# Attention phases of eight scores, with scores and products sharing seven PSUM banks

## The chip, the core and the metric

The kernel runs on one core of one Trainium2 chip. The metric is device time in microseconds (us) of that core; the time before is 1309.45 us, the median of three runs (1308.44 to 1309.51). Five engines run their own instruction streams and meet at semaphores: TensorE (PE in the profile; PEld is its loading of weights), ScalarE (ACT), VectorE (DVE), GpSimd (POOL) and SyncE (SP), which issues the DMAs. Matmul results land in PSUM, which has eight banks of 128 x 512 float32.

## What is computed

One input x (2048 tokens x 512 channels) goes through attention and through a token-mixing MLP, and a gate mixes the two:

```python
qkv = (x @ wqkv)            # 32 heads of 16 channels
p = softmax(q k^T / 4)      # per head, 2048 x 2048
a = (p v) @ wo
h = layernorm(x)
b = (W2 gelu(W1 h^T + b1) + b2)^T     # over the tokens, 1792 hidden
out = g * a + (1 - g) * b   # g = sigmoid(sum(x * gate_w))
```

## The kernel before

The first 300 us project v, q and k, and run the first layer of the MLP. From there to the end of the attention (line 783 to 867) one loop does three things side by side on TensorE: the scores, the products with v, and "dense" matmuls, which are the second MLP layer and later the output projection with wo.

**Groups.** The attention is cut into 32 groups: two halves of the queries (1024 each) times 16 pairs of heads. A group has 64 scores. One score (`score`, the matmul of line 804) is a 128-key by 512-query tile of one head. It uses 64 rows of the array, so a score of head i=0 and one of head i=1 run at the same time on the two halves of the rows; a dense matmul is cut into two halves of 64 rows, which run beside a score in the same way. Two such matmuls that run beside each other are called a slot below.

**From score to product.** Two scores go into one PSUM tile `s` of two banks (three such tiles, line 529). ScalarE takes both in one exponential of 128 x 1024 (line 813) into an SBUF tile `pt`, of which there are six (line 527). Then `apply_v` multiplies by v (line 768): each score gives two matmuls of 17 columns (16 channels and a column of ones for the softmax's sum), 256 wide, on one of four blocks of 32 columns of the array. They add up in one PSUM bank `av` over the whole group (line 531). One more bank, `dn`, holds the dense result.

**Phases.** A group runs in ten phases of six scores and one of four. In a phase TensorE first issues the scores with the dense halves beside them, then all products with v of the *previous* phase's scores. A "two" is a pair of phases; its dense matmuls do one half of their rows in the first phase and the other half in the second. The function `put` deals out how many dense matmuls a two has: 80 of the 160 twos have six (a phase then has six slots), 79 have four (five slots, since two of the six scores then run beside each other) and one has eight. Between the last dense matmul of a phase and the first of the next stands a one-element memset on GpSimd (`token`, line 848).

**Around it.** At the end of a group VectorE copies `av` to the SBUF (`evacuate`, line 731) and later, from a list `slow` that gives out one piece of work per two, takes the reciprocal of the sums (line 742). Both go to DRAM. `fetch_o` (line 596) brings four pairs of heads back, and VectorE multiplies values by reciprocals (line 608) and splits the product in a high and a low part for the output projection. VectorE also evacuates `dn` (lines 513 and 628) and rounds the MLP's weights (line 65), and GpSimd subtracts (line 66). All of these queues are in the order in which the program issues them.

Of the kernel before, what the change touches and what calls it, by code (L numbers as in the profile page):

```python
# [9 lines left out]
F32 = mybir.dt.float32  # L10
# [3 lines left out]
AF = mybir.ActivationFunctionType  # L14
# [7 lines left out]
P = 128  # L22
# [36 lines left out]
def gated_mix(ctx: ExitStack, tc: tile.TileContext, a_x, a_wqkv, a_wo, b_w1, b_b1, b_w2, b_b2, gate_w, out):  # L59
# [3 lines left out]
    def split(hi, lo, src, copy, sub):  # L63

        copy(hi, src)  # L65
        return sub(lo, src, hi.bitcast(F32), ALU.subtract)  # L66
# [456 lines left out]

    o_d = [[dram.tile([P, QW], F32, name=f"o{h}{k}") for k in range(ND)] for h in range(2)]
# [71 lines left out]
    def fetch_o(half, k, pairs=4):  # L596

        n = pairs * 2
        pool, name, bufs = (end, str(k), 1) if half and k > 1 else (o_pool, "", 2)
        rb = pool.tile([P, QW], F32, name=f"o_sum{name}", bufs=1)[: n * DH]  # L600
# [4 lines left out]
        nc.sync.dma_start(rb, r_d[half][k][:n, None, :].broadcast_to([n, DH, QW]))  # L605

        def divide():
            nc.vector.tensor_mul(rb, raw, rb)
            split(hi, lo, rb, nc.vector.tensor_copy, nc.vector.tensor_tensor)

        slow.append((two + 1, divide))
        o_parts[half, k] = hi, lo
# [46 lines left out]
    TWOS = 5  # L659
# [9 lines left out]
    def call(at, *what):  # L669
        calls.setdefault(at, []).append(what)  # L670

    def put_outputs(tiles, n, m, at, sizes=None):
        for t in tiles:
            steps, load = project(t, n, m)
            call(at - 1, load)
            at = put(steps, at, sizes or [m - n])
        return at

    def sizes_of(at, n, fours):

        sizes = [6] * n
        for i in [i for i in reversed(range(n)) if (at + i) % TWOS][:fours]:
            sizes[i] = 4
        return sizes
# [7 lines left out]
    for t in range(NS):  # L692
        if t:
            at = put(second_layer(t), at, sizes_of(at, 9, 6) if t > 9 else sizes_of(at, 8, 3))
# [4 lines left out]
        if t == 10:  # L699
            call(at - 8, fetch_o, 0, 2)  # L700
            call(at - 5, fetch_o, 0, 3)
            at = put_outputs(range(NH), 6, 12, at)
    call(at - 8, fetch_o, 1, 0)
    call(at - 5, fetch_o, 1, 1)
    assert at - 5 > (NP + 8) * TWOS + 4
    call(at, open_end)
    at = put_outputs(range(NS - 3, NS), 0, 4, at)
    assert at == (NP + 12) * TWOS + 7
    call(at - 3, fetch_o, 1, 2)
    at = put_outputs(range(NH, NS - 3), 0, EARLY, at, [4, 4])  # L710
    at = put_outputs(range(NS - 3, NS), 4, EARLY, at)
# [4 lines left out]
    av = ps_av.tile([P, NB], F32, name="av")  # L716
    nc.vector.memset(av, 0.0)
# [7 lines left out]
    def evacuate(g):  # L725
        ot = out_pool.tile([P, NB], F32, name="ot")
        if g == NG - 1:
            for x, y in zip(column_halves(ot), column_halves(av)):
                nc.vector.tensor_scalar_max(x, y, least[0])
            return ot  # L730
        nc.vector.tensor_copy(ot, av)  # L731
# [7 lines left out]
        def invert():  # L739
            rt = out_pool.tile([P, NB], F32, name="rt", bufs=1)  # L740
            nc.vector.tensor_scalar_max(rt, ot, LEAST_SUM)
            nc.vector.reciprocal(rt, rt)  # L742

            def store():
                for rows, cols in blocks:
                    dst = r_d[half][k][None, 2 * p : 2 * (p + 1), cols]
                    nc.sync.dma_start(dst, rt[rows][DH:].rearrange("r (i n) -> r i n", i=2))

            stores.append(store)

        slow.insert(0, (two, invert))

    added = [0, 0]

    def pairs_of(g, units, last):

        pairs = list(zip(*([u for u in units if u[2] == qb] for qb in range(2))))
        return [(g, pair, last and n == len(pairs) - 1) for n, pair in enumerate(pairs)]

    def apply_v(pairs):  # L760
        ot = None
        for g, pair, last in pairs:
            for i, c, qb, pt in pair:

                added[qb] += 1
                for h in range(2):
                    j = 2 * qb + h
                    nc.tensor.matmul(  # L768
                        av[32 * j : 32 * j + VC, i * QC : (i + 1) * QC],
                        v[:, c, g % NP * 2 + i, :],  # L770
                        pt[:, h * QC : (h + 1) * QC],
                        start=added[qb] == 1,
                        stop=added[qb] == 2 * NS,
                    )
            if last:
                added[:] = 0, 0
                ot = evacuate(g)
        return ot

    engines = {getattr(mybir.EngineType, name) for name in ("PE", "Activation", "DVE", "Pool", "SP")}  # L780
    with tc.manual_schedule(engines=engines):
        kt, qt = {0: load_k(0)}, {0: load_q(0)}
        late, open_s, fence = [], None, None
# [9 lines left out]
        def score(grp, i, n, done):  # L793

            nonlocal open_s
            c, qb = n // 2, (n + i) % 2
            if open_s is None:
                open_s = ps_s.tile([P, 2, NB], F32, name="s"), ptp.tile([P, 2, NB], F32, name="pt")
                m = 0
            else:  # L800
                m = 1
            s, pt = open_s
            rows = slice(i * HALF, i * HALF + ROWS)
            nc.tensor.matmul(  # L804
                s[:, m, :],
                kt[grp][rows, c * P : (c + 1) * P],
                qt[grp][rows, qb * NB : (qb + 1) * NB],
                start=True,
                stop=True,
            )  # L810
            done.append((i, c, qb, pt[:, m, :]))
            if m:
                nc.scalar.activation(pt, s, AF.Exp, scale=SCALE)  # L813
                open_s = None

        for grp in range(NG):
            at = [0, 0]
            for ph in range(2 * TWOS + 1):
# [6 lines left out]
                if ph == 2 * TWOS:  # L825
                    n_s, beside = 4, []
                elif second:
                    n_s = 6
                else:
                    for what, *args in calls.get(two, ()):  # L830
                        what(*args)
                    n_s, beside = 6, [step(*args) for step, *args in dense.get(two, ())]
                units = []
                for n in range(n_s - len(beside)):
                    i = (n + second + 1) % 2
                    score(grp, i, at[i], units)
                    at[i] += 1
                half = slice(0, HALF) if second else slice(HALF, P)
                for m, (ps, a, b, first, last, done) in enumerate(beside):

                    if not 4 <= m < len(beside) - 2 or len(beside) <= n_s:
                        score(grp, second, at[second], units)
                        at[second] += 1
# [6 lines left out]
                    if done and second:  # L850
                        done()
                if grp == ph == 0:
                    shift_rows(nc.vector, k_bufs[1])
                if second:
                    while stores:
                        stores.pop()()
                    if len(ready) < 2:
                        split_weight(nc.vector.tensor_copy)
                    for n, (ready_at, step) in enumerate(slow):
                        if ready_at <= two:  # L860
                            slow.pop(n)[1]()
                            break
# [10 lines left out]
    with (  # L873
# [3 lines left out]
        pa = [ps_end.tile([P, D], F32, name=f"pa{t}") for t in range(8)]  # L877
# [153 lines left out]
```

## Time and profile before

| What | Value |
|---|---|
| Median of three runs | 1309.45 us |
| The profiled execution's own time | 1307.55 us |
| Its span, first to last instruction | 1305.8 us |
| Before the attention loop's first score | 303.1 us |
| Attention loop, to the end of the last exponential | 984.2 us |
| After it | 18.4 us |

The profiled execution is 1.9 us under the median and inside 0.15% of it. The profile's page gives busy time of each engine, the chain of work that ended last, and the costliest groups of instructions. In a group's row stand the line, the engine, the operation, output and inputs with their shapes and how often it ran; then the busy time in us and the mean duration in ns, and then the idle time of the engine ahead of it with what ended that. In a timeline each row has the start in us, the time to the end of the last instruction that the row merges, and in brackets the idle time ahead of it. Matmuls overlap in the records, so that TensorE reads as busy nearly all the time; how fast it goes is read from the distance between starts.

### The profile page before, as it was taken

To read this page: it belongs to the slowest core of one execution; us is meant where nothing else is said; L and a number is where in the kernel's file an instruction comes from. 1 tells how busy PE (TensorE), PEld (TensorE's weight loads), DVE (VectorE), ACT (ScalarE), POOL (GpSimd) and SP (SyncE) were. 2 spreads that over 40 slices of the span, in tenths; PEclk is the share of its full clock that TensorE was granted. 3 is DMA by queue.
4 is the path that set the end of the run, shared out by engine and by line. 5 is a ranking of instruction groups with operands and counts; after the bars stand their busy time and mean duration, and the time that the engine had idled before them with its cause. 6 is when DMAs were issued, how large, how long until landed. Compare 5 with 4: busy or idle time off the path is not lost.

```text
span 1305.8 us, 32289 instructions
## 1 busy us (share of the span) xinstructions
PE 1299.0 (99%) x13282; PEld 764.3 (59%) x13282; DVE 403.9 (31%) x538; ACT 1090.6 (84%) x1248; POOL 200.0 (15%) x467
## 2 busy tenths in 40 slices
PE   9999999999999999999999999999999999999998
PEld 7888888886555555555555555555555555454444
DVE  5775361445121111122322111232111111233324
ACT  3443343448999999999999999999999999999994
POOL 0210244453101011011000111100010101100000
PEclk9999999999999999999999999999999999999999
DMA  4497643337443333334655443545433333365522
GB/s 129 144 308 275 229 117 97 97 88 148 75 86 66 62 75 84 69 75 90 126 113 121 82 76 72 120 115 118 79 67 63 74 62 77 75 123 115 112 64 74
DMA packets 93384, 138.41 MB, mean 106 GB/s; under 512 B 14293, under 2 KB 53355, under 8 KB 90156
## 3 DMA queue, kind: packets, MB, share of 16 engines
q1 hardware_dynamic: 92652, 135.20, 44.3%
q8 instruction: 107, 1.75, 0.6%
q10 hardware_dynamic: 576, 1.05, 0.2%
q14 instruction: 49, 0.40, 0.1%
HBM read 99.63 MB, written 36.56 MB: 104 GB/s over the span
## 4 chain that ended last, share of the span: by engine, by line
PE 99%; DVE 0%; issue 0%
PE av L768 37%; PE s L804 29%; PE acc L412 12%; PE acc L73 10%; PE dn L844 10%; PE pa L887 1%; PE acc L184 1%; PE dn L789 0%; PE acc L251 0%; PE acc L228 0%; PE pa L917 0%; DVE base L930 0%; PE pa L895 0%; PE pa L894 0%; DVE idle L223 0%; PE acc L210 0%
## 5 line engine op out<-in xcount | busy, mean ns | idle before, releaser
L813 ACT ACTIVATE pt<-s 128x1024 f32<-128x1024 f32 x1024 | 962.5, 1025 | 20.9 <-PE s L804 14.9
L804 PE MATMUL s<-qs,ks 64*128 64x512 f32 x2048 | 521.3, 420 | 0.0
L768 PE MATMUL av<-pt,v 128*17 128x256 f32 x8192 | 510.6, 381 | 0.0
L804 PEld LDWEIGHTS s<-qs,ks 64*128 64x128 f32 x2048 | 297.6, 184 | 207.6 <-ACT pt L813 182.8
L768 PEld LDWEIGHTS av<-pt,v 128*17 128x17 f32 x8192 | 205.3, 97 | 259.5 <-issue 119.2
L844 PE MATMUL dn<-u_hi,w_hi 64*128 64x512 f32 x428 | 179.6, 420 | 0.0
L844 PE MATMUL dn<-u_hi,w_lo 64*128 64x512 f32 x430 | 170.2, 396 | 0.0
L844 PE MATMUL dn<-u_lo,w_hi 64*128 64x512 f32 x430 | 170.1, 396 | 0.0
L66 POOL TENSOR_TENSOR w_lo<-w_raw,w_hi 128x512 fp32r<-128x512 f32 (+1 forms) x126 | 151.7, 1205 | 115.1 <-ACT w_hi L65 108.5
L848 POOL MEMSET token<- 1x1 f32 x320 | 29.9, 93 | 873.3 <-PE dn L844 704.1
L731 DVE COPY ot<-av 128x512 f32<-128x512 f32 x31 | 21.5, 692 | 344.9 <-PE av L768 344.9
L65 ACT CAST w_hi<-w_raw 128x512 fp32r<-128x512 f32 (+1 forms) x67 | 38.1, 569 | 79.6 <-PE acc L412 58.8
L742 DVE RECIPROCAL rt<-rt 128x512 f32<-128x512 f32 x31 | 104.0, 3353 | 1.1
L412 PE MATMUL acc<-h_hi,w_hi 128*128 128x512 f32 x224 | 87.1, 389 | 0.0
L412 PE MATMUL acc<-h_lo,w_hi 128*128 128x512 f32 x224 | 87.1, 389 | 0.0
L412 PE MATMUL acc<-h_hi,w_lo 128*128 128x512 f32 x224 | 87.1, 389 | 0.0
L65 DVE CAST w_hi<-w_raw 128x512 fp32r<-128x512 f32 (+1 forms) x61 | 23.5, 387 | 190.2 <-PE s L804 82.0
L844 PEld LDWEIGHTS dn<-u_lo,w_hi 64*128 64x128 f32 x430 | 79.5, 185 | 2.5 <-POOL token L848 0.2
L844 PEld LDWEIGHTS dn<-u_hi,w_lo 64*128 64x128 f32 x430 | 79.4, 185 | 2.6
L844 PEld LDWEIGHTS dn<-u_hi,w_hi 64*128 64x128 f32 x428 | 78.8, 184 | 2.2
L73 PE MATMUL acc<-xt_hi,wc_hi 128*128 128x512 f32 x128 | 49.8, 389 | 0.0
L73 PE MATMUL acc<-xt_lo,wc_hi 128*128 128x512 f32 x128 | 49.8, 389 | 0.0
(142 smaller groups left out, 1001.5 us busy)
## 6 DMA issues: line engine op xcount, KB each, us to landing
w_raw<-in_B_w_dram SPq DMA_DIRECT2D x96, 256.0 KB
ks<-kp SPq DMA_DIRECT2D x192, 128.0 KB
qs<-qp SPq DMA_DIRECT2D x256, 64.0 KB
qp<-pc SPq DMA_DIRECT2D x16, 768.0 KB
x<-in_A_x_dram SPq DMA_DIRECT2D x32, 256.0 KB
kp<-pc SPq DMA_DIRECT2D x16, 512.0 KB
w_raw<-in_B_w_dram SPq DMA_DIRECT2D x32, 128.0 KB
bp<-row SPq DMA_DIRECT2D x16, 256.0 KB
```

What stands on the lines that cost most here:

```text
L65: copy(hi, src)
L66: return sub(lo, src, hi.bitcast(F32), ALU.subtract)
L73: nc.tensor.matmul(ps, a, b, start=start and n == 0, stop=stop and n == last)
L184: nc.tensor.transpose(turns[t][:, k, :], xs[t][:, k * P : (k + 1) * P], ident)
L412: nc.tensor.matmul(p, a, b, start=first and k == 0, stop=last and k == 2)
L731: nc.vector.tensor_copy(ot, av)
L742: nc.vector.reciprocal(rt, rt)
L768: nc.tensor.matmul(av[32 * j : 32 * j + VC, i * QC : (i + 1) * QC], v[:, c, g % NP * 2 + i, :], pt[:, h * QC : (h + 1) * QC], start=added[ ...
L804: nc.tensor.matmul(s[:, m, :], kt[grp][rows, c * P : (c + 1) * P], qt[grp][rows, qb * NB : (qb + 1) * NB], start=True, stop=True,)
L813: nc.scalar.activation(pt, s, AF.Exp, scale=SCALE)
L844: mm = nc.tensor.matmul(ps, a[half], b[half], start=first and not second, stop=last and bool(second))
L848: fence = nc.gpsimd.memset(token, 0.0)
```

## The change

Phases have eight scores, and a group has eight of them (`TWOS = 4`, `N_S = 8`). A two has six or eight dense matmuls and none has four. There are 128 twos; 18 of them have eight dense matmuls and 110 have six, so 36 phases have eight dense halves (eight slots) and 220 have six (seven slots, the first with two scores beside each other).

The three two-bank tiles and the bank `av` become one tile of seven banks. A table `TURN` says for each of eight phases, which repeat, into which banks its eight scores go and into which bank the products of that phase go. Two scores in neighbouring banks are taken by one exponential of 128 x 1024. In every fourth phase the last two scores are not neighbours and are taken by two exponentials of 128 x 512. The products of one phase are added up in their bank, and VectorE then adds that bank to an SBUF tile `ot` (`sums`), which GpSimd has set to zero at the start of the group. Only the parts of the bank that the phase has written are added: in a phase with six dense halves two instructions (128 x 256 and 64 x 256), with eight one (128 x 256). The copy at the group's end goes. `reads` and `writes` set the waits by bank: a matmul waits for what last read its bank, a reader waits for the matmuls that wrote it.

The reciprocals are cut in two halves, and the division of `fetch_o` in two pieces; `slow` is now looked at once per phase, and not in phases that round weights or end a dense tile. The output projection is dealt out in 24 runs instead of 27. The pool of `pt` tiles keeps its six tiles.

```diff
+    RING = 7
+    TURN = [
+        ((3, 4, 5, 6, 0, 1, 2, 3), 4),
+        ((5, 6, 0, 1, 2, 3, 4, 5), 6),
+        ((0, 1, 2, 3, 4, 5, 6, 0), 1),
+        ((4, 5, 2, 3, 0, 6, 1, 5), 4),
+    ]
+    TURN += [(tuple(RING - 1 - s for s in scores), RING - 1 - b) for scores, b in TURN]
...
     ptp = ptp_ctx.enter_context(tc.tile_pool(name="pt", bufs=6, reuse_waits="tile"))
-    ps_s = psum_ctx.enter_context(tc.tile_pool(name="ps_s", bufs=3, space=PSUM, reuse_waits="tile"))
+    ps_s = psum_ctx.enter_context(tc.tile_pool(name="ps_s", bufs=1, space=PSUM, reuse_waits="tile"))
-    ps_av = psum_ctx.enter_context(tc.tile_pool(name="ps_av", bufs=1, space=PSUM, reuse_waits="tile"))
...
-        slow.append((two + 1, divide))
+        slow.append((two + 1, lambda: nc.vector.tensor_mul(rb, raw, rb)))
+        slow.append((two + 1, lambda: split(hi, lo, rb, nc.vector.tensor_copy, nc.vector.tensor_tensor)))
...
-    TWOS = 5
+    TWOS = 4
+    N_S = 8
...
+    banks = ps_s.tile([P, RING, NB], F32, name="s")
...
+    def reads(ins, *at):
...
+        for bank in at:
+            readers[bank].append(ins)
+            for mm in writers[bank].values():
+                tc.add_manual_dep(ins.ins, mm.ins.name, SYNC, reason="the bank is written")
+
+    def writes(mm, bank, block=0, source=None):
...
+        for ins in readers[bank]:
+            tc.add_manual_dep(mm.ins, ins.ins.name, SYNC, reason="the bank is read")
+        readers[bank].clear()
...
+    def apply_v(late, bank, end=False):
...
+        pairs = [sorted(units[n : n + 2], key=lambda u: u[2]) for n in range(0, N_S, 2)]
+        av = banks[:, bank, :]
...
+        for x, y in parts:
+            reads(nc.vector.tensor_tensor(x, y, x, ALU.add), bank)
...
+            beside = [m for m, unit in enumerate(units) if unit[3] is None and abs(turn[m] - bank) == 1]
+            if beside:
+                exponentials(turn, units, [sorted((beside[0], len(units) - 1), key=lambda m: turn[m])])
+            elif len(units) == N_S:
+                exponentials(turn, units, [[m] for m, unit in enumerate(units) if unit[3] is None])
+
+        def exponentials(turn, units, runs):
+            pt = ptp.tile([P, 2, NB], F32, name="pt")
...
+                act = nc.scalar.activation(dst, banks[:, at[0] : at[-1] + 1, :], AF.Exp, scale=SCALE)
+                reads(act, *at)
...
-            for ph in range(2 * TWOS + 1):
+            for ph in range(2 * TWOS):
+                if ph == 0:
+                    sums[grp] = out_pool.tile([P, NB], F32, name="ot")
+                    nc.gpsimd.memset(sums[grp], 0.0)
...
+                turn, av_bank = TURN[(2 * two + second) % len(TURN)]
...
-                n = 2 if ph == 2 * TWOS and grp < NG - 1 else len(late)
-                apply_v(late[:n])
-                late = late[n:] + pairs_of(grp, units, ph == 2 * TWOS)
-        last_ot = apply_v(late)
+                apply_v(late, av_bank)
+                if grp and not ph:
+                    store_sums(grp - 1)
+                late = grp, units
```

More of the change, by code (lines that the diff above doesn't have):

```diff
@@ L1 @@
+from collections import deque
 from contextlib import ExitStack
@@ L598, in fetch_o @@
         n = pairs * 2
-        pool, name, bufs = (end, str(k), 1) if half and k > 1 else (o_pool, "", 2)
-        rb = pool.tile([P, QW], F32, name=f"o_sum{name}", bufs=1)[: n * DH]
+        assert stored.issuperset(half * NP + 4 * k + p for p in range(pairs))
+        pool, name, bufs = (end, str(k), 1) if half else (o_pool, "", 2)
+        rb = pool.tile([P, QW], F32, name="o_sum", bufs=1)[: n * DH]
         hi = pool.tile([P, QW], F32R, name=f"o_hi{name}", bufs=bufs)[: n * DH]
@@ L723, in column_halves, with store_sums @@
         return x[:, 0], x[:, 1]
[L725 to L731, printed above, removed]
+    def store_sums(g):
+        ot = sums.pop(g)
         half, p = divmod(g, NP)
@@ L737, in evacuate, with invert, store @@
             nc.sync.dma_start(dst, ot[rows][:DH].rearrange("r (i n) -> r i n", i=2))
[L739 to L765, printed above, removed]
+        rt = []
+        def invert(i):
+            if not rt:
+                rt.append(out_pool.tile([P, NB], F32, name="rt", bufs=1))
+            cols = slice(i * QC, (i + 1) * QC)
+            nc.vector.tensor_scalar_max(rt[0][:, cols], ot[:, cols], LEAST_SUM)
+            nc.vector.reciprocal(rt[0][:, cols], rt[0][:, cols])
+        def store():
+            stored.add(g)
+            for rows, cols in blocks:
+                dst = r_d[half][k][None, 2 * p : 2 * (p + 1), cols]
+                nc.sync.dma_start(dst, rt[0][rows][DH:].rearrange("r (i n) -> r i n", i=2))
+        slow[:0] = (two, lambda: invert(0)), (two, lambda: (invert(1), stores.append(store)))
+    def apply_v(late, bank, end=False):
+        if not late:
+            return
+        g, units = late
+        pairs = [sorted(units[n : n + 2], key=lambda u: u[2]) for n in range(0, N_S, 2)]
+        av = banks[:, bank, :]
+        taken = [0, 0]
+        for pair in pairs:
+            for i, c, qb, pt, act in pair:
+                taken[qb] += 1
                 for h in range(2):
                     j = 2 * qb + h
-                    nc.tensor.matmul(
+                    mm = nc.tensor.matmul(
                         av[32 * j : 32 * j + VC, i * QC : (i + 1) * QC],
@@ L851, in gated_mix @@
                         done()
+                if splits:
+                    split_weight(nc.vector.tensor_copy)
                 if grp == ph == 0:
                     shift_rows(nc.vector, k_bufs[1])
[L854 to L862, printed above, removed]
-                n = 2 if ph == 2 * TWOS and grp < NG - 1 else len(late)
-                apply_v(late[:n])
-                late = late[n:] + pairs_of(grp, units, ph == 2 * TWOS)
-        last_ot = apply_v(late)
+                apply_v(late, av_bank)
+                if grp and not ph:
+                    store_sums(grp - 1)
+                late = grp, units
+        assert not slow and not stores
+        last_ot = sums[NG - 1]
+        apply_v(late, TURN[0][1], end=True)
     psum_ctx.close()
@@ L876, in gated_mix @@
     ):
-        pa = [ps_end.tile([P, D], F32, name=f"pa{t}") for t in range(8)]
+        pa = {t: ps_end.tile([P, D], F32, name=f"pa{t}") for t in (7, 2, 4, 6, 1, 3, 5, 0)}
         LATE = 3, 5, 7
```

129 lines of the change are left out of this document (70 added, 59 removed).

## The prediction

> **What bounds the kernel now.** I read the page first (sections 1, 2, 4 and 5), then busy time by stage, then the waits of ScalarE and of the weight loads, then the timeline of three neighbouring phases on TensorE and ScalarE.
>
> ```profile
> span 1305.8 us, 32289 instructions
> PE 1299.0 (99%) x13282; PEld 764.3 (59%) x13282; DVE 403.9 (31%) x538; ACT 1090.6 (84%) x1248; POOL 200.0 (15%) x467
> PEclk9999999999999999999999999999999999999999
> PE 99%; DVE 0%; issue 0%
> L813 ACT ACTIVATE pt<-s 128x1024 f32<-128x1024 f32 x1024 | 962.5, 1025 | 20.9 <-PE s L804 14.9
> ```
> ```profile
> 303.20:1287.40 984.20, 984.20 (x11840) 508.11 (x11840) 229.34 (x241) 963.06 (x1025) 100.89 (x381) 1.00 0.43 88
> 1287.40:1305.80 18.40, 12.77 (x95) 8.72 (x92) 11.03 (x16) 1.09 (x2) 1.29 (x1) 0.92 0.34 120
> ```
>
> The chain is TensorE throughout, at full granted clock. The stage row is the attention loop: 984.2 us, columns PE, PEld, DVE, ACT, POOL. ScalarE is busy 963 us of it, so two engines are close to full, and a change in how they wait for each other decides. VectorE has 755 us free.
>
> The timeline of TensorE from 856.20 holds a phase with five slots, the group's four-score phase and one with six slots; below it is ScalarE.
>
> ```profile
> 856.20 0.50 PE L804 MATMUL s<-qs,ks 64*128 64x512 f32 x2
> 856.54 0.63 PE L804 MATMUL s<-qs,ks 64*128 64x512 f32 x2
> 857.01 0.40 PE L804 MATMUL s<-qs,ks 64*128 64x512 f32 x1
> 857.24 0.39 PE L804 MATMUL s<-qs,ks 64*128 64x512 f32 x1
> 857.57 1.49 PE L768 MATMUL av<-pt,v 128*17 128x256 f32 x24
> 858.99 0.73 PE L804 MATMUL s<-qs,ks 64*128 64x512 f32 x4
> 859.66 1.06 PE L768 MATMUL av<-pt,v 128*17 128x256 f32 x16
> 860.64 0.50 PE L804 MATMUL s<-qs,ks 64*128 64x512 f32 x1
> 862.25 1.49 PE L768 MATMUL av<-pt,v 128*17 128x256 f32 x24
> 863.67 0.49 PE L804 MATMUL s<-qs,ks 64*128 64x512 f32 x1
> ```
> ```profile
> 856.80 1.03 ACT L813 ACTIVATE pt<-s 128x1024 f32<-128x1024 f32 x1
> 861.47 2.86 ACT L813 ACTIVATE pt<-s 128x1024 f32<-128x1024 f32 x3
> 864.49 1.02 ACT L813 ACTIVATE pt<-s 128x1024 f32<-128x1024 f32 x1 [0.17 <-PE s L804]
> ```
>
> From these starts: five slots take 858.99 - 856.20 = 2.79 us, six take 863.67 - 860.64 = 3.03, the four-score phase 1.65. With 160, 159 and 31 of them that is 485 + 444 + 51 = 980 us, the stage within half a per cent: TensorE sets the pace of every phase. ScalarE does three exponentials in 2.86 us, an interval of (2.86 - 1.03) / 2 = 0.915, or 2.75 per phase, and then waits for the next phase's first scores (0.17 idle at 864.49). Its queue never runs dry for longer, and TensorE waits for no bank for long, since a score's bank was read by the exponential three before.
>
> **The change, part by part.** *TensorE's own work.* Slots start 0.23 apart after a first one of 0.34 (856.20, 856.54; 857.01, 857.24), and the products follow the last slot's start by 0.33 (857.24 to 857.57). The products of six scores take 1.42 (857.57 to 858.99), of four 0.98, so eight take 1.42 + 0.43 = 1.85. A phase of seven slots is then 1.37 (five slots) + 2 x 0.23 + 1.85 = 3.68, one of eight 3.91. With 220 and 36 phases: 810 + 141 = 951 us, 33 less than now; this is what going from 352 phases to 256 takes off the switches between scores and products. Matmul counts stay.
>
> *ScalarE's own work.* 256 phases of four intervals are 937 us. The 64 phases with two exponentials of 512 columns have no row. From the rows below, 512 columns take 0.59 to 0.69 us where 1024 take 1.03; bounds for the interval are 0.46 (half of 0.915) and 0.69 (no overlap). I take 0.50, as the shorter row saves 0.44 of 1.03 and 0.915 - 0.44 = 0.48. A pair then costs 0.085 more than one of 1024 (bounds 0 and 0.47): 5 us, so 942.
>
> ```profile
> L65 ACT CAST pc<-acc 128x512 fp32r<-128x512 f32 x32 | 18.7, 585 | 23.8 <-PE acc L73 19.3 <-DMA qp<-pc 4.6
> L351 ACT ACTIVATE pc<-acc,kmax 128x512 fp32r<-128x512 f32 x16 | 11.0, 689 | 14.2 <-DVE pc L66 14.2
> ```
>
> Either engine alone would be faster than 984. But the table adds two waits between them, and both lie on a loop that closes once per phase.
>
> *The eighth score's bank.* In every row of `TURN` the eighth score goes into a bank of the first pair (3 in 3,4; 5 in 5,6; 0 in 0,1; 5 in 4,5). It waits for the first exponential of its own phase. The latencies stand in these rows:
>
> ```profile
> 500.00 1.93 ACT L813 ACTIVATE pt<-s 128x1024 f32<-128x1024 f32 x2
> 501.98 0.18 PEld L804 LDWEIGHTS s<-qs,ks 64*128 64x128 f32 x1 [0.19 <-ACT pt L813]
> 502.08 0.40 PE L804 MATMUL s<-qs,ks 64*128 64x512 f32 x1
> 502.65 0.63 PE L768 MATMUL av<-pt,v 128*17 128x256 f32 x8
> ```
>
> An exponential ends at 501.93, the score that waited starts at 502.08: 0.15. Seven slots: the first exponential starts 0.60 after the phase (856.20 to 856.80), ends at 1.63, and lets the eighth score start at 1.78. Its slot would come at 1.37 - 0.33 + 2 x 0.23 = 1.50, so TensorE stands 0.28 us, with a dense half and all products queued behind. The phase becomes 1.78 + 0.33 + 1.85 = 3.96. With eight slots the first pair needs two slots, the exponential starts at 0.83 (860.64 to 861.47), and the phase is 0.83 + 1.03 + 0.15 + 0.33 + 1.85 = 4.19. This wait alone: 220 x 3.96 + 36 x 4.19 = 1022 us.
>
> *The `pt` tiles.* There are still six, but a phase now fills four. The third exponential writes the tile that the first one of the phase before filled, and that tile is read by the first two scores' products, which TensorE issues after the eighth score. Before, three tiles per phase left a whole phase of room. Now the third exponential starts after: first exponential 1.03, eighth score 0.15, products 0.33, their first two scores' share 0.63 (the eight matmuls at 502.65), and 0.10 from a matmul's end to ScalarE's start (856.20 + 0.50 to 856.80). That is 2.24 us after the first exponential, against 1.83 without the wait. Then two intervals until the next phase's first one: 2.24 + 1.83 = 4.07, and I use 4.06, since each row is rounded to 0.01. This loop is longer than the 3.96, so it holds for seven slots; for eight slots 4.19 stays. Phases with the two short exponentials: 4.06 + 0.09 = 4.15.
>
> *VectorE.* The seventh score's bank is the one that the last products were in, so it waits for the additions.
>
> ```profile
> L908 DVE TENSOR_TENSOR sums<-ot,sums 128x256 f32<-128x256 f32 x1 | 0.4, 411 | 0.0
> L729 DVE TENSOR_SCALAR ot<-av,least 128x256 f32<-128x256 f32 x2 | 0.9, 480 | 3.8 <-PE av L768 3.8
> L731 DVE COPY ot<-av 128x512 f32<-128x512 f32 x31 | 21.5, 692 | 344.9 <-PE av L768 344.9
> L742 DVE RECIPROCAL rt<-rt 128x512 f32<-128x512 f32 x31 | 104.0, 3353 | 1.1
> 1145.32 0.63 SPq L605 DMA_DIRECT2D o_sum<-r  x1
> 1157.55 1.22 DVE L608 TENSOR_TENSOR o_sum<-o_lo,o_sum 128x1024 f32<-128x1024 f32 x1 [10.27 <-DMA o_sum<-r]
> ```
>
> Products end 0.07 after the next phase starts (857.57 + 1.49 against 858.99). Two additions of 0.41 (bound: 0.69, the copy of 512 columns) at 0.48, the row that reads the same bank with 256 columns, end at 0.07 + 0.10 + 0.96 = 1.13, and the score could start at 1.28. It may start as late as 1.55 without moving the eighth. So the additions cost nothing, with 0.27 us of cover; each 0.1 beyond it costs 22 us over 220 phases. The halved reciprocal (1.7 us) is issued after an addition and is over before the next. `fetch_o` is the exception: its data took 12.2 us (1145.32 to 1157.55), while the multiplication may be issued one two, 8.1 us, after the DMA. With its 1.22 us the addition would be up to 12.2 + 1.2 - 8.1 - 4.1 = 1.2 late, so eight fetches cost 0 to 8 us; I take 0. The 31 copies that go (0.69 each) were idle time of VectorE, and the 32 memsets on GpSimd run a phase ahead of their use: nothing. SP issues about as many DMAs as before, in longer phases: nothing.
>
> *The sum.* 165 x 4.06 + 55 x 4.15 + 36 x 4.19 = 670 + 228 + 151 = 1049 us, against 984: +65. What stands before the loop and after it keeps its instructions. The profiled execution had 1307.55 us (span 1305.8); 1372.5 is its new time, and the median, 1.9 above it, gives 1374 us.
>
> **Rivals.** *No wait binds* (faster): the first exponential ends before the eighth slot and TensorE sets the pace: 951 us, 1276. For it: TensorE has been the chain all along, and its work falls. Against it: 1.63 + 0.15 against 1.50, from rows that repeat in every phase. It decides at 984 / 256 = 3.84 us per phase: the wait would have to shrink from 0.28 to 0.16 and the tile wait vanish. The Trainium skill's page "Perfetto Trace Analysis", section "Matmuls", speaks for this rival: groups should rotate through the banks so that an evacuation overlaps the next group's matmuls; by that rule the 951 would be the sum.
>
> *The tile wait does not bind*: the third exponential finds its tile free, and 1022 us remain, +38: 1347. For it: TensorE may stand less than computed and start the products sooner. Against it: the order of issue, eighth score before products.
>
> *VectorE is late*: additions of 0.69 instead of 0.48 put the seventh score at 1.70, 0.15 past its cover: +33 us, 1407. For it: 128 x 512 took 0.69 whether copied or subtracted; against it: half the columns took 0.41 to 0.48.
>
> *The clock falls.* TensorE now stands some 0.4 us in every phase. The granted clock is 9 in all slices, and no stretch of this trace stands like that. If a tenth of the phases ran at half clock (3.68 more each), that is +94 us: 1468. The Trainium skill's page "TensorE: Matmul & The Clock Gate", section "A second HAM failure mode: psum-queue depth-cycling", reports such a fall for a kernel that cycles through banks.
>
> **How the numbers follow.** Forecast 0.72 at 1374; no tile wait 0.08 at 1347; VectorE late 0.10, up to 1407; clock 0.02; no wait at all 0.06 at 1276; close to no change 0.02. The range 1345 to 1405 reaches to the second and third and leaves out a little over one in ten. Its ends also hold the bounds of the short exponentials (-5 to +25 us) and of the fetches. 0.2%, 2.6 us, is about what a measurement of this kernel can tell from no change: faster 0.06, same 0.01, slower 0.93.
>
> **What would show it.** In the changed profile the exponentials of 1024 columns have some 100 us idle ahead of them, released by products (the third of each phase); starts in a phase are 0.9, 1.3, 0.9 and 0.9 us apart; the loads of scores wait for ScalarE in mid-phase, 0.2 to 0.3 us some 250 times; the stage is near 1049 us. It is wrong if seven-slot phases come every 3.7 us (no wait), if the idle time ahead of the exponentials is small, or if scores wait for VectorE.

## The result and the profile after

The changed kernel takes 1392.72 us (median of four runs, 1389.72 to 1393.37), the kernel before took 1308.95 us beside it (1308.12 to 1309.51): a ratio of 1.0636, with a 95% interval of 1.0618 to 1.0654. It is 84 us slower; the forecast was 1374 us, with 1345 to 1405 as its range.

The page of the changed kernel, first the span, the busy times, the granted clock and the chain, then the groups of the exponentials (line 850 now) and of the additions (line 809):

```profile
span 1387.9 us, 32932 instructions
...
PE 1371.2 (99%) x13282; PEld 776.8 (56%) x13282; DVE 592.8 (43%) x1040; ACT 1100.2 (79%) x1312; POOL 207.3 (15%) x435
...
PEclk9999999999999999999999999999999999999999
...
PE 94%; DMA 3%; SPq 1%; DVE 1%; ACT 0%; issue 0%; DVEq 0%
...
L850 ACT ACTIVATE pt<-s 128x1024 f32<-128x1024 f32 (+1 forms) x1088 | 972.2, 981 | 92.9 <-PE s L789 71.5
...
L809 DVE TENSOR_TENSOR ot<-s,ot 128x256 f32<-128x256 f32 x476 | 202.8, 426 | 573.2 <-PE s L789 530.1
```

The attention loop as one stage, after and then before, in the order PE, PEld, DVE, ACT, POOL, clock, DMA share, GB/s:

```profile
304.70:1369.10 1064.40, 1055.36 (x11834) 519.86 (x11834) 418.30 (x742) 972.18 (x1088) 106.65 (x347) 1.00 0.38 79
```
```profile
303.90:1287.40 983.50, 983.50 (x11836) 507.55 (x11832) 228.64 (x240) 962.56 (x1025) 100.19 (x381) 1.00 0.43 87
```

The loop has grown by 80.9 us, the span by 82.1. ScalarE does 972 us of work in a stage of 1064, so it now stands 92 us where it stood 21: 92.9 idle ahead of the exponentials against 20.9, and 71.5 of that ended by products (line 789). PE still reads 99% busy, which says little, since matmuls that overlap in the records also count as busy while TensorE is fed slowly. The waits say more:

```profile
PEld s L829 <- ACT pt L850: 292.8, 737, 0.6
ACT pt L850 <- PE s L789: 71.5, 199, 4.3
DVE o_sum L619 <- DMA o_sum<-r: 16.0, 4, 5.5
```

The loads of scores wait for ScalarE and ScalarE waits for products: the two engines wait for each other by turns. The timeline of two neighbouring phases, TensorE from one phase's start to the next, then one load of weights from the same phase, and ScalarE below:

```profile
570.84 0.50 PE L829 MATMUL s<-qs,ks 64*128 64x512 f32 x2
...
572.31 0.39 PE L829 MATMUL s<-qs,ks 64*128 64x512 f32 x1
...
572.66 0.50 PE L829 MATMUL s<-qs,ks 64*128 64x512 f32 x1
...
573.09 1.92 PE L789 MATMUL s<-pt,v 128*17 128x256 f32 x32
574.94 0.50 PE L829 MATMUL s<-qs,ks 64*128 64x512 f32 x2
```
```profile
571.74 0.18 PEld L829 LDWEIGHTS s<-qs,ks 64*128 64x128 f32 x1 [0.37 <-ACT pt L850]
```
```profile
569.75 3.78 ACT L850 ACTIVATE pt<-s 128x1024 f32<-128x1024 f32 x4 [0.32 <-PE s L789]
573.84 3.77 ACT L850 ACTIVATE pt<-s 128x1024 f32<-128x1024 f32 x4 [0.32 <-PE s L789]
```

Phases come 574.94 - 570.84 = 4.10 us apart. Each of ScalarE's rows holds four exponentials that run back to back, from a phase's third to the next phase's second, and ahead of each third one are 0.32 us of waiting for products. The eighth score (572.66) starts 0.35 after the seventh, not 0.23. The fifth is held up too: its load (571.74) waits until the fourth exponential of the phase before has left its bank, and it starts 0.32 after the slot before. The slot behind each of the two waits is 0.10 late as well. The median distance over all phases is 4.095 us with seven slots, 4.15 with the two short exponentials and 4.18 with eight slots; 4.06, 4.15 and 4.19 were forecast.

Three phases are not like the others: they take 6.1, 8.5 and 8.9 us, 11 us more than three ordinary ones. The timeline of the second of them, over SP, VectorE and TensorE:

```profile
1239.13 0.63 SPq L617 DMA_DIRECT2D o_sum<-r  x1
...
1249.56 1.23 DVE L619 TENSOR_TENSOR o_sum<-o_lo,o_sum 128x1024 f32<-128x1024 f32 x1 [5.54 <-DMA o_sum<-r]
1250.81 0.88 DVE L809 TENSOR_TENSOR ot<-s,ot 128x256 f32<-128x256 f32 x2
...
1251.75 0.79 PE L829 MATMUL s<-qs,ks 64*128 64x512 f32 x1 [3.03 <-DVE ot L809]
...
1252.90 2.77 PE L789 MATMUL s<-pt,v 128*17 128x256 f32 x32
```

VectorE stands 5.54 us at the multiplication of `fetch_o`, whose data are still on their way, and the additions stand behind it in its queue. The score that needs the additions' bank waits with them: TensorE stands 3.03 us. Then the 32 products take 2.77 us instead of 1.92. The stage view of these microseconds shows why; the last column but two is the granted clock:

```profile
1246.00:1250.00 4.00, 2.72 (x34) 1.15 (x25) 0.44 (x1) 3.76 (x4) 0.00 (x0) 1.00 0.66 164
1250.00:1254.00 4.00, 2.25 (x16) 0.99 (x20) 3.84 (x6) 0.00 (x0) 0.09 (x1) 0.66 0.09 34
1254.00:1258.00 4.00, 3.99 (x46) 1.98 (x42) 1.32 (x3) 3.75 (x4) 0.09 (x1) 0.92 0.62 207
1258.00:1262.00 4.00, 4.00 (x50) 1.92 (x46) 0.85 (x2) 3.68 (x6) 0.00 (x0) 1.00 0.58 169
```

After the stand the clock is down, to 0.66 and 0.92 of full speed, and it is back at 1.00 in the last row.

### The profile page after: what moved, and what is told of

It is laid out like the page before. It is cut to its first block, busy times and chain, and to the rows that moved or that the text cites. A ratio compares the mean times of both kernels' runs of the same rounds, so it can differ in the third digit from the quotient of the medians.

```text
span 1387.9 us, 32932 instructions
## 1 busy us (share of the span) xinstructions
PE 1371.2 (99%) x13282; PEld 776.8 (56%) x13282; DVE 592.8 (43%) x1040; ACT 1100.2 (79%) x1312; POOL 207.3 (15%) x435
## 4 chain that ended last, share of the span: by engine, by line
PE 94%; DMA 3%; SPq 1%; DVE 1%; ACT 0%; issue 0%; DVEq 0%
PE s L789 33%; PE s L829 32%; PE acc L413 11%; PE acc L74 9%; PE dn L895 8%; DMA o_sum<-r 2%; PE pa L934 1%; PE acc L185 0%; SPq L499 0%; PE acc L252 0%; DMA x<-in_A_x_dram 0%; DMA qs<-qp 0%; DMA ks<-kp 0%; DVE o_sum L619 0%; ACT pt L850 0%; PE pa L964 0%
## 5 line engine op out<-in xcount | busy, mean ns | idle before, releaser
L850 ACT ACTIVATE pt<-s 128x1024 f32<-128x1024 f32 (+1 forms) x1088 | 972.2, 981 | 92.9 <-PE s L789 71.5
L829 PE MATMUL s<-qs,ks 64*128 64x512 f32 x2048 | 598.3, 441 | 6.4 <-DVE ot L809 5.0
L789 PE MATMUL s<-pt,v 128*17 128x256 f32 x8192 | 492.9, 381 | 0.0
L809 DVE TENSOR_TENSOR ot<-s,ot 128x256 f32<-128x256 f32 x476 | 202.8, 426 | 573.2 <-PE s L789 530.1
L789 PEld LDWEIGHTS s<-pt,v 128*17 128x17 f32 x8192 | 215.5, 97 | 214.5 <-issue 64.2
L895 PE MATMUL dn<-u_hi,w_lo 64*128 64x512 f32 x430 | 206.5, 480 | 0.0
L895 PE MATMUL dn<-u_hi,w_hi 64*128 64x512 f32 x428 | 170.2, 398 | 0.0
L899 POOL MEMSET token<- 1x1 f32 x256 | 22.8, 89 | 936.5 <-PE dn L895 936.5
L765 DVE RECIPROCAL rt<-rt 128x256 f32<-128x256 f32 x62 | 108.7, 1753 | 2.1
L66 ACT CAST w_hi<-w_raw 128x512 fp32r<-128x512 f32 (+1 forms) x67 | 38.1, 569 | 79.4 <-PE acc L413 58.8
L74 PE MATMUL acc<-xt_hi,wc_lo 128*128 128x512 f32 x128 | 49.8, 389 | 0.0
```

The source lines that it names most:

```text
L74: nc.tensor.matmul(ps, a, b, start=start and n == 0, stop=stop and n == last)
L765: nc.vector.reciprocal(rt[0][:, cols], rt[0][:, cols])
L789: mm = nc.tensor.matmul(av[32 * j : 32 * j + VC, i * QC : (i + 1) * QC], v[:, c, g % NP * 2 + i, :], pt[:, h * QC : (h + 1) * QC], start=t ...
L809: reads(nc.vector.tensor_tensor(x, y, x, ALU.add), bank)
L829: mm = nc.tensor.matmul(banks[:, bank, :], kt[grp][rows, c * P : (c + 1) * P], qt[grp][rows, qb * NB : (qb + 1) * NB], start=True, stop=True,)
L850: act = nc.scalar.activation(dst, banks[:, at[0] : at[-1] + 1, :], AF.Exp, scale=SCALE)
```

## The experiments

The theory was the forecast's: two waits that close once per phase, the longer through the `pt` tiles, the shorter through the eighth score's bank, and fetches on top. The rivals: that VectorE's additions hold the bank, and that TensorE has become slower by its short stands (the clock). The table gives each kernel's median over that of the kernel before beside it (1308.95 for the change, 1307.88 for split_first, seven_tiles, no_additions and later_division, 1308.37 for the rest), and from the traces the median distance of the seven-slot phases.

| Kernel | Median, us | Over before, us | Ratio (95%) | Seven slots, us |
|---|---|---|---|---|
| the change | 1392.72 | +83.8 | 1.0636 (1.0618 to 1.0654) | 4.095 |
| split_first | 1340.70 | +32.8 | 1.0249 (1.0232 to 1.0266) | 3.865 |
| seven_tiles | 1364.67 | +56.8 | 1.0434 (1.0417 to 1.0452) | 3.96 |
| no_additions | 1383.50 | +75.6 | 1.0572 (1.0554 to 1.0589) | 4.095 |
| later_division | 1387.31 | +79.4 | 1.0604 (1.0587 to 1.0622) | 4.095 |
| split_seven | 1319.62 | +11.3 | 1.0088 (1.0073 to 1.0104) | 3.75 |
| fetch_early | 1378.64 | +70.3 | 1.0535 (1.0519 to 1.0551) | 4.095 |
| split_seven_fetch | 1300.34 | -8.0 | 0.9941 (0.9928 to 0.9955) | 3.75 |
| five_tiles | 1613.81 (one run) | +305 | 1.2335 | 5.01 |

**seven_tiles** gives `pt` a seventh tile, so that the exponential that waits for the first products is the fourth of a phase and no longer the third. The room for it comes from two other pools.

```diff
-    ptp = ptp_ctx.enter_context(tc.tile_pool(name="pt", bufs=6, reuse_waits="tile"))
+    ptp = ptp_ctx.enter_context(tc.tile_pool(name="pt", bufs=7, reuse_waits="tile"))
...
-            raw = wk.tile([P, NB], F32, name="w_raw", bufs=4)
+            raw = wk.tile([P, NB], F32, name="w_raw", bufs=3)
...
-        bp = out_pool.tile([P, D], F32, name="row", bufs=3)
+        bp = out_pool.tile([P, D], F32, name="row", bufs=2)
```

> Seven pt tiles instead of six (room for it from one row tile and one w_raw tile less). Loop theory: the third exponential finds its tile free and the wait of the eighth score is left: 3.96 to 4.0 per seven-slot phase, the short pairs cost nothing, eight slots stay at 4.18: 25 to 35 us less, 1360 to 1368. Rivals, ScalarE's own work or VectorE's additions: no change, 1393.

TensorE's timeline over the same phase of this kernel:

```profile
571.62 0.50 PE L829 MATMUL s<-qs,ks 64*128 64x512 f32 x2
...
573.30 0.50 PE L829 MATMUL s<-qs,ks 64*128 64x512 f32 x1
...
573.74 1.92 PE L789 MATMUL s<-pt,v 128*17 128x256 f32 x32
575.59 0.50 PE L829 MATMUL s<-qs,ks 64*128 64x512 f32 x2
```

575.59 - 571.62 = 3.97: the 3.96 that the forecast had for the bank's wait alone. Eight-slot phases stay at 4.18. The kernel gains 27 us, although four phases are now long, 4.6 to 9.4 us, 15 us over ordinary ones instead of 11. One of the two smaller pools also has a price of its own, which shows under split_seven_fetch.

**five_tiles** goes the other way, from six tiles to five and nothing else. The exponential that waits is then the second of a phase.

```diff
-    ptp = ptp_ctx.enter_context(tc.tile_pool(name="pt", bufs=6, reuse_waits="tile"))
+    ptp = ptp_ctx.enter_context(tc.tile_pool(name="pt", bufs=5, reuse_waits="tile"))
```

> Five pt tiles instead of six. Loop theory: now the second exponential waits for the first products of the phase before, 2.27 us after the first one, and three intervals follow: 2.27 + 3 x 0.915 = 5.0 per phase or more where short pairs come in, over 0.9 more than with six: 1560 to 1640. Rivals, ScalarE's own work or VectorE's additions as the bound: 1393 or little more.

ScalarE's timeline, then the loop as a stage:

```profile
571.48 3.77 ACT L850 ACTIVATE pt<-s 128x1024 f32<-128x1024 f32 x4 [1.23 <-PE s L789]
576.50 3.84 ACT L850 ACTIVATE pt<-s 128x1024 f32<-128x1024 f32 x5 [1.24 <-PE s L789]
```
```profile
304.70:1590.00 1285.30, 1131.17 (x11786) 521.44 (x11786) 417.95 (x740) 966.54 (x1085) 106.30 (x347) 1.00 0.32 66
```

From one waiting exponential to the next are 5.02 us. That is the 4.10 of six tiles and one interval (0.915) more, as a loop must give in which three exponentials instead of two follow the waiting one; 222 us more than the change are 0.87 for each of 256 phases. TensorE reads as idle for 154 of the 1285 us, in some 500 stands of which the longest is 1.9 us, and the granted clock is 1.00 over the whole loop: stands this short don't bring it down here.

**split_first** takes the other wait away from its root. Where the table has the pair of the eighth score's bank, the first pair's exponential of 1024 columns becomes two of 512, and the one whose bank the eighth score takes runs first.

```diff
-                exponentials(turn, units, [sorted((beside[0], len(units) - 1), key=lambda m: turn[m])])
+                pair = sorted((beside[0], len(units) - 1), key=lambda m: turn[m])
+                if beside[0] == 0:
+                    exponentials(turn, units, [[m] for m in sorted(pair, key=lambda m: turn[m] != turn[-1])])
+                else:
+                    exponentials(turn, units, [pair])
```

> Each phase's first pair of scores is taken by two exponentials of 512 columns, the one first whose bank the eighth score takes; the rest is as in the changed kernel. Loop theory (the eighth score waits for the first exponential, the third exponential for its tile): the bank is free at 0.60 + 0.59 + 0.15 = 1.34 us, before the eighth slot at 1.50; products start at 1.83, the third pair's exponential at 1.83 + 0.73 = 2.56, the next phase's first one two intervals later, 3.82 per seven-slot phase and 3.91 with eight slots. Against 4.10 and 4.18 now that is about 70 us less: 1320 to 1330. Rival, ScalarE's own work is the bound: 256 more short exponentials cost 0.04 per phase, 10 us more: 1403. Rival, VectorE's additions hold the phases: no change, 1393.

One of the waits, then the groups of the exponentials by form, and then rows of one phase: the dense halves beside the fourth, fifth, sixth and eighth score, and the products:

```profile
PEld s L789 <- ACT pt L854: 91.6, 252, 0.4
```
```profile
L854 ACT ACTIVATE pt<-s 128x1024 f32<-128x1024 f32 x704 | 707.4, 1035 | 24.2 <-issue 14.8 <-PE s L789 2.1 <-ACT pt L854 1.0
L854 ACT ACTIVATE pt<-s 128x512 f32<-128x512 f32 x640 | 342.7, 610 | 3.7 <-PE s L829 3.4 <-ACT pt L854 0.2
```
```profile
571.76 0.39 PE L899 MATMUL dn<-u_lo,w_hi 64*128 64x512 f32 x1
572.08 0.49 PE L899 MATMUL dn<-u_hi,w_lo 64*128 64x512 f32 x1
572.42 0.39 PE L899 MATMUL dn<-u_hi,w_hi 64*128 64x512 f32 x1
...
572.88 0.40 PE L899 MATMUL dn<-u_hi,w_lo 64*128 64x512 f32 x1
573.21 1.92 PE L789 MATMUL s<-pt,v 128*17 128x256 f32 x32
```

The idle time ahead of the exponentials falls from 92.9 to 28 us, while their busy time as one group grows from 972.2 to 988.3 us. Products end only 2.1 us of it, so the sooner eighth score also brings the first products forward, and with them the tile: this one edit loosens both loops, and the kernel gains 51 us. The median lies 10.7 us above the range expected. Phases were expected at 3.82 and take 3.865. The view of the waits names the loads of the products (252 times for ScalarE), but the products are not late: they start 573.21 - 572.88 = 0.33 after the eighth slot, as they did in the kernel before. What is late is the fifth score. It goes into a bank of the last pair of the phase before, waits for that pair's exponential, and starts 0.32 after the slot before; the next one follows 0.34 later (572.08, 572.42). Without a wait both steps would be 0.23, so 0.2 us go here, and TensorE's own 3.68 become 3.87. This third wait is in the loop of the tiles: from a third exponential to its fourth 0.92, the fourth's 1.03, the fifth score 0.05 behind its end, the eighth 0.34 + 2 x 0.23 later, then 0.33, 0.63 and 0.10 to the next third exponential, 3.86 in all. The other part of the miss is in the long phases: they now take 10.1, 10.1, 10.5 and 5.2 us, 20 us more than ordinary ones instead of 11.

**no_additions** keeps the additions of one phase in eight and leaves out the others, so that the products of those phases don't reach the output. It asks whether VectorE sets any phase.

```diff
-        for x, y in parts:
+        for x, y in parts if add else []:
...
-                apply_v(late, av_bank)
+                apply_v(late, av_bank, add=not ph)
```

> VectorE adds only the last phase's products of each group; the products of the other seven phases are left out of the output. Loop theory: the phases keep 4.10 us, and only what stood behind the fetched data goes (the three phases that were 2.0, 4.3 and 4.8 us longer), 5 to 11 us less: 1382 to 1388. Rival, VectorE's additions hold the phases: the phases become shorter by up to 0.4 us, 1290 to 1340.

The group of the long exponentials:

```profile
L850 ACT ACTIVATE pt<-s 128x1024 f32<-128x1024 f32 x960 | 917.5, 1031 | 86.8 <-PE s L789 83.1 <-PE s L829 3.7
```

Ordinary phases stay at 4.095 us, and ScalarE still waits 83 us for products. The additions cost nothing in them. Most of the 8 us gained are in the long phases, of which two are left with 7.41 and 5.51 us; there the evacuation of `dn` stands behind the multiplication instead of the additions.

**later_division** only moves the multiplication of `fetch_o` and its split one phase pair later, except for the last fetch, whose data are needed soon after.

```diff
-        slow.append((two + 1, lambda: nc.vector.tensor_mul(rb, raw, rb)))
+        at = two + (1 if half and k == 3 else 2)
+        slow.append((at, lambda: nc.vector.tensor_mul(rb, raw, rb)))
```

> The multiplication of fetched values by the reciprocals may be issued two twos after the fetch instead of one (the last fetch stays). Loop theory with the fetch as its own term: the three long phases go, 11 us less, 1382; all other phases stay at 4.10. If the three long phases have another cause, no change: 1393.

The timeline of SP and VectorE near the end of the loop:

```profile
1280.99 0.62 SPq L617 DMA_DIRECT2D o_sum<-r  x1
1281.65 0.46 SPq L634 DMA_DIRECT2D row<-part  x1
...
1288.54 0.75 DVE L638 SCALAR_TENSOR_TENSOR row<-dn,g,row 128x512 f32<-128x512 f32 x1 [7.58 <-DMA row<-part]
```

Two of the three long phases are gone, but the third grew to 13.09 us, and only 4 us of the expected 11 or so came. `o_sum` is one tile. The next fetch can't be issued before the late split has read it, SP's queue stands there, and the fetch of `row` behind it on SP comes late too: VectorE waits 7.58 us for it, with `dn` full. So the wait now ends at the rows behind the fetch in SP's queue.

**fetch_early** mends that: two places for `o_sum` in turn, and the fetches some phases sooner, beside the later division.

```diff
-        rb = pool.tile([P, QW], F32, name="o_sum", bufs=1)[: n * DH]
+        rb = (o_pool if k % 2 else pool).tile([P, QW], F32, name="o_sum", bufs=1)[: n * DH]
...
-    call(at - 8, fetch_o, 0, 2)
-    call(at - 5, fetch_o, 0, 3)
+    call(at - 12, fetch_o, 0, 2)
+    call(at - 6, fetch_o, 0, 3)
...
-    for k, n in enumerate((1, 3, 5)):
+    for k, n in enumerate((1, 2, 4)):
```

> The changed kernel with the moved fetches alone (12 and 6 twos ahead, then 1, 2 and 4, two tiles in turn, division two twos later). The three long phases (11 us) go: 1381 to 1384; the other phases stay at 4.10. If what blocked the queue of SP with the later division comes back, 1387.

No phase is long any more, no wait for `o_sum` is left, and the ordinary phases stay at 4.095. It gains 13.5 us over the change, and its median lies 2.4 us below the range expected: 11 were the excess of the long phases, and the other 2.5 lie within the intervals of the two ratios.

**split_seven** has both edits, the split first pair and the seventh tile.

```diff
-    ptp = ptp_ctx.enter_context(tc.tile_pool(name="pt", bufs=6, reuse_waits="tile"))
+    ptp = ptp_ctx.enter_context(tc.tile_pool(name="pt", bufs=7, reuse_waits="tile"))
...
+                    exponentials(turn, units, [[m] for m in sorted(pair, key=lambda m: turn[m] != turn[-1])])
```

> First pair in two short exponentials and seven pt tiles together. Loop theory: neither wait is left on the loop; TensorE's 3.68 (3.91 with eight slots) and ScalarE's 3 x 0.915 + 2 x 0.477 = 3.70 (3.74 where the last pair is short too) are the bound, and as both are full at once some 0.05 is lost: 3.75 and 3.93. That is 0.11 less than with the split alone: 1312 to 1320, with the long phases of the fetches (about 20 us) still in it. Rival: a third wait of the same size as the two (the seventh score for the additions) then takes over, phases stay at 3.86, 1340.

The median phase is 3.75 us, as expected, and half of all phases lie between 3.73 and 3.80. The fifth score starts 0.23 after the slot before again, so its wait is gone with the seventh tile, and the rival of a third wait that stays has fallen. The kernel is 11 us from the one before. What is left are long phases, 10.2, 11.4, 11.3 and 5.2 us. One of them in the timeline (TensorE and ScalarE), and TensorE's clock in stretches of it:

```profile
1222.59 0.76 PE L899 MATMUL dn<-wo_hi,o_hi 64*128 64x512 f32 x1 [4.30 <-DVE row L637]
...
1225.41 3.47 PE L789 MATMUL s<-pt,v 128*17 128x256 f32 x32
1226.60 1.08 ACT L854 ACTIVATE pt<-s 128x512 f32<-128x512 f32 x2 [1.19 <-PE s L789]
```
```profile
1218.00:1220.00 2.00, 0.29 (x3) 0.00 (x0) 0.00 (x0) 1.25 (x3) 0.00 (x0) 1.00 0.65 181
1220.00:1222.00 2.00, 0.00 (x0) 0.00 (x0) 1.54 (x2) 0.00 (x0) 0.00 (x0) 0.94 0.16 60
1222.00:1224.00 2.00, 1.41 (x6) 1.25 (x8) 1.90 (x5) 0.54 (x1) 0.00 (x0) 0.50 0.69 208
...
1226.00:1228.00 2.00, 2.00 (x28) 0.73 (x20) 0.00 (x0) 1.08 (x2) 0.00 (x0) 0.50 0.00 0
```

TensorE stands 4.30 us for a `dn` tile that VectorE empties late, and then works at half clock for about 6 us: its products take 3.47 us instead of 1.92.

**split_seven_fetch** puts the edits of fetch_early on top.

```diff
-        rb = pool.tile([P, QW], F32, name="o_sum", bufs=1)[: n * DH]
+        rb = (o_pool if k % 2 else pool).tile([P, QW], F32, name="o_sum", bufs=1)[: n * DH]
...
-    call(at - 8, fetch_o, 0, 2)
+    call(at - 12, fetch_o, 0, 2)
```

> As split_seven, with the fetches of the first half's values 12 and 6 twos ahead of their use instead of 8 and 5, those of the second half 1, 2 and 4 twos after the MLP's end with two tiles in turn, and the division two twos after the fetch. Loop theory: the long phases go, some 20 us off split_seven: 1292 to 1300, faster than the kernel before by 10 to 15 us. Rival, the fetch's wait only moves to the SP queue and to the rows loaded behind it: 1310 to 1320.

The loop and the stage behind it:

```profile
305.70:1276.80 971.10, 967.12 (x11831) 520.38 (x11828) 419.18 (x744) 965.24 (x1345) 106.46 (x347) 1.00 0.43 87
1276.80:1298.50 21.70, 13.15 (x104) 9.04 (x100) 10.58 (x15) 1.09 (x2) 1.29 (x1) 0.85 0.28 101
```

This is the first of these kernels that beats the one before, by 8 us: 1300.34 us, 0.9941 of it (0.9928 to 0.9955). The loop is 12.4 us shorter than before. That is what eight scores per phase are worth here once the tiles and the first pair's bank stand in the way no longer and the fetches hardly do. VectorE waits for no `o_sum` any more, but three phases are still long, 5.25, 4.68 and 5.17 us, 4 us more than ordinary ones. In them VectorE waits for a row that SP loads late, and TensorE for `dn`:

```profile
DVE row L638 <- DMA row<-part: 6.9, 3, 3.6
PE dn L900 <- DVE row L638: 2.7, 3, 1.1
```

So the rival came true in a small part. SP's loads of rows wait 27 us in this kernel for stores out of the same tiles, 22 us in seven_tiles, and less than 1 us in the change: the `row` pool gave one of its three tiles to the seventh `pt` tile. That these 4 us would go with a third `row` tile is likely, but no run shows it.

The median lies 0.3 us above the range expected. What follows the loop takes 21.7 us where the change has 18.8. VectorE's last addition ends 13.9 us after the loop in both, so the difference lies behind it, where the last rows are stored; its cause stays open.

## Why the prediction was right, and where it was short

*Both waits.* Right in the mechanism. The loop through the `pt` tiles was forecast as 2.24 us from the first exponential to the third and two intervals of 0.915. Measured: the waiting exponentials come 4.09 apart, which less 2 x 0.915 leaves 2.26. That it came out so near is in part luck, since two errors nearly cancel in its pieces. The eighth score starts about 0.09 sooner after the first exponential than worked out: the 0.15 was read from the matmul at 502.08, which started one ordinary slot of 0.23 after the one at 501.85 and so did not stand at all, while a score that stands starts 0.05 after the exponential's end (the row of the kernel before stands below). And the products follow it by 573.09 - 572.66 = 0.43, not 0.33, since the step behind a stand is 0.10 longer. The 3.96 of the bank's wait alone has the same two errors in it (1.68 for 1.78 to the eighth score, 0.44 for 0.33 behind it). The wait of the fifth score was missing; with six tiles it takes 0.19 of the 0.41 us by which a phase exceeds TensorE's own work, and the eighth score the other 0.22. One tile more gave the 3.96 of the other wait alone, one tile less one interval more. The 27 us that the seventh tile gained answer to the 27 between the forecast and its own rival without a tile wait.

```profile
501.85 0.39 PE L804 MATMUL s<-qs,ks 64*128 64x512 f32 x1
```

*No wait binds.* The rival failed for this kernel, and its number (951 us for the loop) is the goal that the edited kernels come near: 971 with the waits and most of the fetches' cost out of the way. Its condition, under 3.84 us per phase, is met there, and the kernel is faster than before. The sentence of the Trainium skill that stood beside it (the page "Perfetto Trace Analysis", section "Matmuls", on rotating groups through the banks) doesn't decide here: the banks do rotate, but seven of them serve nine uses in a phase, and the tiles behind them six for four.

*VectorE is late.* Right to be set at nothing in ordinary phases: 426 ns per addition, and no change of the phase without them.

*Fetches.* This is the step that failed. "Eight fetches cost 0 to 8 us; I take 0" was 11 us, on three phases. The time of the data was not the error: where VectorE waited it was 6.9 to 12.1 us from the DMA's issue to the multiplication, and 12.2 had been allowed for. The distance was. The forecast has the multiplication 8.1 us behind the DMA; in the four fetches that made VectorE wait, VectorE came to it 7.7, 6.2, 4.9 and 2.1 us after the DMA, because SP issued the DMA late. SP's queue had been put at nothing, but in two of the four it stands until VectorE has split the fetch before, which is in the same tile `o_sum`:

```profile
SPq L617 <- DVE o_lo L67: 14.3, 2, 9.1
```

The forecast also had only the stand itself in its cost. TensorE stands 1.9, 3.0 and 3.2 us in the three phases, 8.1 in all, and the remaining 3 us are from after the stands, where the granted clock is below 1.00.

*The clock.* The rival had TensorE's short stands in many phases bring it down. That fell: with 0.4 us lost in each phase, and with 1.3 in five_tiles (5.01 against 3.68), the clock is 1.00. But it does fall after a single long stand. The Trainium skill's page "TensorE: Matmul & The Clock Gate", section "HAM oscillation — how this bites in real kernels", gives some 3.4 us of idleness as the bound; here 1.93 us left the clock at 1.00, and 3.03 and 4.30 us were followed by rows below it. The 3.03 are idle time after a matmul's recorded end; from that matmul's start to the next they are 3.42 us (1248.33 to 1251.75), so these runs don't tell whether the bound lies lower. The fall that the prediction cites from that page's section on depth-cycling was seen in none of these runs.

*The sum.* Of the 18.7 us between forecast and median, the profiled run shows most. Its loop grew by 80.9 us, not by 65: 11 of these 16 us are the fetches, and nearly 5 are the seven-slot phases, which take 4.105 us in the mean where the forecast's average was 4.08. The rest of the span grew by 1.2 us. The median lies 3.0 us above the profiled run, where the forecast took over the 1.9 of the kernel before. Of the signs that were named, the idle time ahead of the exponentials (92.9 for "some 100"), its releaser and the distances in a phase came as said; the loads of scores waited 204 times and 110 us more than before, where "some 250 times" at 0.2 to 0.3 us were named. Among these are the fifth scores.

## What to carry to other kernels

Between two engines that are both near full, count for every pool on the way how many phases pass from a tile's filling to its last reading and compare that with its tiles; the wait that closes last sets the phase, whatever the busy shares say, and when it is taken away, the next one does: here the tiles, then the fifth score's bank, then the work itself. Bring such a loop down at its head: the first exponential of half the size, run first, gave 51 us, the seventh tile alone 27. When an engine that used to have slack comes onto that loop, look through its queue for anything that waits for a DMA, since that wait is now everybody's, and through the DMA queue for what holds up that DMA's issue.

## What was not expected of the hardware

An exponential of 512 columns takes 0.61 us where one of 1024 takes 1.03, but the next one starts 1.08 - 0.61 = 0.47 us later in the row above, and 0.48 in the median of split_first, close to half of 0.915. Cutting one in two thus costs about 0.04 us of ScalarE, and frees the first bank 0.4 us sooner.

A stand of TensorE can cost more than its length. The one of 1.93 us lengthened its phase by its own length; those of 3.03 and 3.2 us cost 1.4 and 1.6 us more, and that of 4.30 us 3.2 more. After it the clock was at 0.50 for about 6 us, and 32 products took 3.47 instead of 1.92 us. Where phases became shorter, the same fetches took about as long from issue to use (6.9 to 12.1 us in the change, 7.3 to 12.9 in split_seven), so VectorE waited longer for them, up to 7.1 us instead of 5.5, and the long phases went from 8.9 us at most to 11.4.
